# The linear part of an MLP, associated the other way: (h w_in) first instead of w_in (alpha w_out)

## The chip, the cores and the metric

The kernel runs on one core of a Trainium2 chip. The time is device microseconds of one execution; the median of 3 runs is shown. Engines: PE is TensorE, ACT ScalarE, DVE VectorE, POOL GpSimd, SP the engine that issues the DMAs.

## What is computed

The input x has 12480 rows (tokens) of 128 values. An attention with 32 inducing rows comes first, then two MLPs with 2048 hidden values:

```python
h = mab(I, x)                  # 32 rows attend to all of x: h is 32 x 128
x = mab(x, h)                  # each token attends to the 32 rows: a @ h, a is 12480 x 32
h1 = x @ w_in                                                    # first MLP
x = (np.maximum(h1, 0) + alpha * np.minimum(h1, 0)) @ w_out
r = np.maximum(x @ w2_in, 0)                                     # second MLP
out = (r * r) @ w2_out
```

`mab` is softmax(q kv^T / sqrt(128)) kv. All is fp32; w_in, w_out, w2_in and w2_out come as float64 and alpha has 2048 values.

## The kernel before

The first MLP's activation is split as alpha h1 + (1 - alpha) max(h1, 0). The second part needs the hidden layer; the first one is linear. With x = a h, the linear part is a V with V = h w_in diag(alpha) w_out, a matrix of 32 x 128 that is made once. `aw` holds first (1 - alpha) w_out, which is split in a high and a low part (`wo_hi`, `wo_lo`), and later alpha w_out.

*Stage 1* (to about 38 us) reads x, transposes it and gathers h over tokens. h is kept transposed and four times side by side: `hT`, 128 x 128 (L429). During this stage w_in is brought to fp32 (`w_in_sb`), and w_out behind it in four pieces (`convs[4]` to `convs[7]`: ACT, ACT, DVE, DVE and POOL, then `rest` and `split`).

*Between the stages* stand the scores and softmax of token tile 0 (`first`, steps 0 to 7) and of tiles 1 to 3 (`second`, steps 0 to 6), and `make_w1s(k)`: four products that give w1s = h w_in, 512 columns each. In the kernel before, PE also transposes the 16 chunks of w_in (`transpose_w_in(0..3)`, L388 to L393), and ACT copies them to `wiT`.

*The main loop* goes over s = 0 to 479. Step s computes chunk c = s mod 16 of token tile s // 16. `l1_a` multiplies a tile's attention weights `a_s` with w1s, ACT and DVE make the high and low part of max(h1, 0) (`g1h`, `g1l`); some steps later `l1_b` multiplies them with `wo_hi` and `wo_lo`, three products, and adds them up in a bank `y`. From step 24 on `l2_a`, `l2_split` and `l2_b` do the second MLP, whose weights arrive and are converted in eight pieces during the first steps (`PIECES`). Each engine works in order, and the order is written out by hand: `at(s, f)` hangs f behind step s. So were hung, in the kernel before:

- `second[2]` to `second[6]` (softmax of tiles 1 to 3) at steps 0, 2, 2, 4 and 7. `second[6]` makes `a_hi` on ACT and `a_lo` on POOL, and twelve DMAs on SP copy them to `a_s` of three tiles. Behind these twelve in SP's queue stands the load of the first piece of w2_out (step 9).
- `make_w1s(2)` at step 2 and `make_w1s(3)` at step 5.
- The scaling of `aw` by alpha on ACT (L219) at steps 8, 7, 16 and 15 (`AW`), and `step_u(0..3)` at steps 16 to 19: u = w_in (alpha w_out), 16 products summed in one bank.
- `copy_u` on ACT at 19, `step_v` at 20 (the product of `hT` and u on PE, L580, then `v_s` on ACT and DVE), and `end_y1(0)` at 22, which adds a V to tile 0 and is the first to read `v_s`.

PSUM has eight banks by name: h1 two, h2 two, y1 one, y2 two, ms one. Banks of one name are used in turn, and a new use waits until the last reader of the use before it (two uses before, for a pair) is done.

Of the kernel before, what the change touches and what calls it, by code (L numbers as in the profile page):

```python
# [9 lines left out]
F32 = mybir.dt.float32  # L10
# [3 lines left out]
AF = mybir.ActivationFunctionType  # L14
ALU = mybir.AluOpType
# [10 lines left out]
Q = 4  # L26
# [3 lines left out]
def attention_then_two_mlps(ctx: ExitStack, tc, x, inducing, w_in, w_out, alpha, w2_in, w2_out, out):  # L30
# [13 lines left out]
    scale = 1.0 / math.sqrt(C)  # L44
# [6 lines left out]
    keep = ctx.enter_context(tc.tile_pool(name="keep", bufs=1))  # L51
# [21 lines left out]
    def keep_tile(name, shape, dt=F32):  # L73
        return keep.tile(shape, dt, name=name, tag=name)
# [8 lines left out]
    def st_tile(name, shape):  # L83
        return st.tile(shape, F32, name=name, tag=name)
# [11 lines left out]

    ident = cv.tile([P, P], F32, name="ident", tag="u_sb", bufs=1)
    make_identity(nc, ident)  # L100

    same = st_tile("same", [P, P])
    nc.gpsimd.memset(same, 0.0)
    for k in range(-(Q - 1), Q):
        nc.gpsimd.affine_select(
# [19 lines left out]

    w_in_sb = keep.tile([P, DFF], F32, name="w_in_sb", tag="w2i_hi")
    w_out_sb = keep.tile([P, NCH, P], F32, name="w_out_sb", tag="w2i_lo")
    wiT = keep.tile([P, DFF], F32, name="wiT", tag="w2o_hi")
    aw = keep.tile([P, NCH, P], F32, name="aw", tag="w2o_lo")
    al = keep_tile("al", [P, NCH])  # L130
    al1 = keep_tile("al1", [P, NCH])
# [43 lines left out]
    def to_f32(name, k, place):  # L175

        v = {}  # L180
# [27 lines left out]
    def conv_w_out(k):  # L208
        chunks, cols = slice(4 * k, 4 * k + 4), slice(k * 512, (k + 1) * 512)
        f, hi, lo, a = (v.rearrange("p c d -> p (c d)")[:, cols] for v in (w_out_sb, wo_hi, wo_lo, aw))  # L210

        def rest():
            nc.gpsimd.tensor_tensor(
                aw[:, chunks], w_out_sb[:, chunks], al1[:, chunks].unsqueeze(2).to_broadcast([P, 4, P]), op=ALU.mult
            )

        def scaled():
            for c in range(4 * k, 4 * k + 4):
                nc.scalar.activation(aw[:, c, :], w_out_sb[:, c, :], AF.Copy, scale=al[:, c : c + 1])  # L219

        def split():
            nc.scalar.copy(hi, a)
            pool_lo(lo, a, hi)


        return to_f32("w_out", k, lambda: f) + [rest, split, scaled]

    def conv_w2(name, k, hi, lo):
        f = []
# [129 lines left out]
    b = free_bank()  # L359
# [25 lines left out]
            nc.vector.tensor_copy(al, b[:, :NCH])  # L385
            nc.vector.tensor_scalar(al1, al, -1.0, 1.0, op0=ALU.mult, op1=ALU.add)

    def transpose_w_in(k):  # L388
        b = y2_bank()
        for i in range(4):  # L390
            c = 4 * k + i
            nc.tensor.transpose(b[:, i * P : (i + 1) * P], w_in_sb[:, c * P : (c + 1) * P], ident)
        nc.scalar.copy(wiT[:, k * 512 : (k + 1) * 512], b)  # L393


    b = scores(last)
    values1(last - 1)
    maxima(last, b)
# [24 lines left out]
    den = st.tile([P, M], F32, name="den", tag="den")  # L423
    nc.vector.tensor_scalar_add(den, d[:, :M], 1e-9)
    nc.vector.reciprocal(den, den)
    transpose_w_in(0)
    b = y1_bank()
    nc.tensor.matmul(b[:, :P], h_run, sel, start=True, stop=True)
    nc.vector.tensor_tensor(  # L429
        hT.rearrange("c (q j) -> c q j", q=Q), b[:, :P].rearrange("c (q j) -> c q j", q=Q),  # L430
        den.unsqueeze(1).to_broadcast([P, Q, M]), op=ALU.mult,
    )
    transpose_w_in(1)
    run(convs[5][2:4])
    convs[4][4]()

# [99 lines left out]
    second = second_attention([1, 2, 3])  # L536
    first[0]()
    make_w1s(0)
    transpose_w_in(2)
    run(convs[6][:2])  # L540
    run(first[1:4])
    split_w1s(0, 0)
    second[0]()
    transpose_w_in(3)
    stage1.close()
    make_w1s(1)
    convs[5][4]()
# [12 lines left out]

    u_bank = []

    def step_u(k):
        if k == 0:
            u_bank.append(y2_bank())
        for c in range(4 * k, 4 * k + 4):
            nc.tensor.matmul(
                u_bank[0][:, :P], wiT[:, c * P : (c + 1) * P], aw[:, c, :], start=(c == 0), stop=(c == NCH - 1)  # L570
            )

    u_sb = cv.tile([P, P], F32, name="u_sb", tag="u_sb", bufs=1)

    def copy_u():
        nc.scalar.copy(u_sb, u_bank[0][:, :P])

    def step_v():
        bv = free_bank()
        nc.tensor.matmul(bv[:, :P], hT, u_sb, start=True, stop=True)  # L580
        nc.scalar.copy(v_s, bv[:, :P])
        nc.vector.tensor_tensor(v_s[64:], bv[64:, :P], f32(v_s[64:]), op=ALU.subtract)

# [98 lines left out]
    def at(s, f, *a):  # L682
        plan.setdefault(s, []).append(lambda: f(*a))
# [108 lines left out]
```

## Time and profile before

| | us |
|---|---|
| median of 3 runs | 978.12 (977.93 to 978.18) |
| the profiled execution | 976.3 |
| its span, first to last instruction | 974.2 |
| PE busy in the span | 957.3 (98%) |
| ACT busy | 756.1 (78%) |
| DVE busy | 671.8 (69%) |
| POOL busy | 543.7 (56%) |

The times in a timeline count from the span's start. Where a row carries "[1.29 <-ACT u_sb L576]", the engine had been idle for 1.29 us before it, and what ended this was that instruction. Matmuls overlap, so that the duration of one is longer than its distance to the next. An f32 product is two passes in the timeline. Buffer numbers are left out of names, so the arrays of the second MLP (`moe2`) read like those of the first.

### The profile page before, as it was taken

To read this page: it belongs to the slowest core of one execution; us is meant where nothing else is said; L and a number is where in the kernel's file an instruction comes from. 1 tells how busy PE (TensorE), PEld (TensorE's weight loads), DVE (VectorE), ACT (ScalarE), POOL (GpSimd) and SP (SyncE) were. 2 spreads that over 40 slices of the span, in tenths; PEclk is the share of its full clock that TensorE was granted. 3 is DMA by queue.
4 is the path that set the end of the run, shared out by engine and by line. 5 is a ranking of instruction groups with operands and counts; after the bars stand their busy time and mean duration, and the time that the engine had idled before them with its cause. 6 is when DMAs were issued, how large, how long until landed. Compare 5 with 4: busy or idle time off the path is not lost.

```text
span 974.2 us, 15106 instructions
## 1 busy us (share of the span) xinstructions
PE 957.3 (98%) x5023; PEld 879.7 (90%) x5023; DVE 671.8 (69%) x1129; ACT 756.1 (78%) x1500; POOL 543.7 (56%) x484
## 2 busy tenths in 40 slices
PE   9889999999999999999999999999999999999997
PEld 7568999998999989999999999899998999999997
DVE  5778876666766667666677666676666766666677
ACT  5689887777877777777788777787777787777775
POOL 2358765555665555655556555566555665555530
PEclk9999999999999999999999999999999999999999
DMA  9531002000020000110000200002000010000001
GB/s 327 155 101 59 9 3 46 11 10 1 10 48 10 1 10 10 30 20 10 10 10 3 46 11 10 1 11 48 10 1 10 10 34 16 10 10 10 1 10 20
DMA packets 65838, 28.36 MB, mean 29 GB/s; under 512 B 53968, under 2 KB 61664, under 8 KB 65760
## 3 DMA queue, kind: packets, MB, share of 16 engines
q1 hardware_dynamic: 64832, 27.29, 11.3%
q8 instruction: 39, 0.64, 0.3%
q14 instruction: 39, 0.32, 0.1%
q10 hardware_dynamic: 928, 0.11, 0.1%
HBM read 14.80 MB, written 6.39 MB: 22 GB/s over the span
## 4 chain that ended last, share of the span: by engine, by line
PE 93%; DMA 2%; DVE 2%; ACT 2%; issue 1%; SPq 0%; ACTq 0%; DVEq 0%
PE y L604 18%; PE y L605 18%; PE y L606 18%; PE h L604 9%; PE h L606 9%; PE h L605 9%; PE h L594 9%; DMA xg<-in_x_dram 2%; PE y L622 1%; PE ms L453 1%; DVE g1l L600 1%; DMA raw<-in_moe_w_out_dram 0%; ACT g1h L598 0%; PE h L262 0%; PE ms L276 0%
## 5 line engine op out<-in xcount | busy, mean ns | idle before, releaser
L649 POOL TENSOR_TENSOR g2l<-sq,g2h 128x448 fp32r<-128x448 f32 (+1 forms) x424 | 486.4, 1148 | 343.8 <-ACT g2h L647 336.5
L600 DVE SCALAR_TENSOR_TENSOR g1l<-h,g1h 128x448 fp32r<-128x448 f32 (+1 forms) x448 | 277.3, 620 | 226.0 <-ACT g1h L598 220.6
L598 ACT ACTIVATE g1h<-h 128x448 fp32r<-128x448 f32 (+1 forms) x448 | 243.7, 545 | 135.4 <-PE h L594 131.7
L640 DVE TENSOR_TENSOR sq<-h,r 128x448 f32<-128x448 f32 (+1 forms) x448 | 278.1, 621 | 49.0 <-ACT r L638 4.8
L638 ACT ACTIVATE r<-h 128x448 f32<-128x448 f32 (+1 forms) x448 | 244.5, 546 | 54.2 <-PE h L606 8.7
L647 ACT CAST g2h<-sq 128x448 fp32r<-128x448 f32 (+1 forms) x448 | 249.4, 557 | 1.8 <-DVE sq L640 1.5
L594 PE MATMUL h<-a_s,w1s 128*128 128x448 f32 (+1 forms) x448 | 164.6, 368 | 4.8 <-DVE g1l L600 3.1
L604 PE MATMUL h<-y1h,w2i_hi 128*128 128x448 f32 (+1 forms) x448 | 162.8, 363 | 0.1
L606 PE MATMUL y<-g1l,wo_hi 128*128 128x448 f32 (+1 forms) x448 | 162.4, 363 | 0.0
L606 PE MATMUL h<-y1l,w2i_hi 128*128 128x448 f32 (+1 forms) x448 | 162.2, 362 | 0.2 <-DVE y1l L626 0.2
L604 PE MATMUL y<-g1h,wo_hi 128*128 128x448 f32 (+1 forms) x448 | 162.4, 362 | 0.0
L605 PE MATMUL y<-g1h,wo_lo 128*128 128x448 f32 (+1 forms) x448 | 162.3, 362 | 0.0
L606 PE MATMUL y<-g2l,w2o_hi 128*128 128x448 f32 (+1 forms) x448 | 162.2, 362 | 0.0
L604 PE MATMUL y<-g2h,w2o_hi 128*128 128x448 f32 (+1 forms) x448 | 162.2, 362 | 0.0
L605 PE MATMUL y<-g2h,w2o_lo 128*128 128x448 f32 (+1 forms) x448 | 162.1, 362 | 0.0
L605 PE MATMUL h<-y1h,w2i_lo 128*128 128x448 f32 (+1 forms) x448 | 162.1, 362 | 0.0
L594 PEld LDWEIGHTS h<-a_s,w1s 128*128 128x128 f32 (+1 forms) x448 | 84.1, 188 | 17.3 <-DVE g1l L600 6.3
L604 PEld LDWEIGHTS h<-y1h,w2i_hi 128*128 128x128 f32 x448 | 84.1, 188 | 7.2 <-DVE sq L640 1.4
L604 PEld LDWEIGHTS y<-g1h,wo_hi 128*128 128x128 f32 x448 | 84.4, 188 | 5.6 <-issue 0.5
L606 PEld LDWEIGHTS h<-y1l,w2i_hi 128*128 128x128 f32 x448 | 84.1, 188 | 5.8 <-DVE y1l L626 0.5
L606 PEld LDWEIGHTS y<-g2l,w2o_hi 128*128 128x128 f32 x448 | 84.1, 188 | 5.7 <-DVE g2l L649 0.2
L604 PEld LDWEIGHTS y<-g2h,w2o_hi 128*128 128x128 f32 x448 | 84.1, 188 | 5.6
(124 smaller groups left out, 723.0 us busy)
## 6 DMA issues: line engine op xcount, KB each, us to landing
out_dram<-o SPq DMA_DIRECT2D x106, 56.0 KB, 1.9
xg<-in_x_dram SPq DMA_DIRECT2D x10, 512.0 KB, 8.8
raw<-in_moe_w_in_dram SPq DMA_DIRECT2D x8, 512.0 KB, 6.3
raw<-in_moe_w_out_dram SPq DMA_DIRECT2D x8, 512.0 KB, 4.2
a_s<-a_hi SPq DMA_DIRECT2D x54, 56.0 KB, 1.9
a_s<-a_lo SPq DMA_DIRECT2D x54, 56.0 KB, 1.9
xg<-in_x_dram SPq DMA_DIRECT2D x4, 256.0 KB, 4.2
out_dram<-o SPq DMA_DIRECT2D x4, 48.0 KB, 1.8
```

The costliest lines, as they stand in the source:

```text
L453: nc.tensor.matmul(b[i * M : (i + 1) * M, :w], hT[:, :M], rhs, start=True, stop=True, tile_position=(0, i * M),)
L594: nc.tensor.matmul(b[:, :w], w1s[: a.shape[0], c * P : (c + 1) * P], a, start=True, stop=True)
L598: nc.scalar.activation(hi, b[:, :w], AF.Relu)
L600: nc.vector.scalar_tensor_tensor(lo, b[:, :w], 0.0, f32(hi), op0=ALU.max, op1=ALU.subtract)
L604: nc.tensor.matmul(b, w_hi, hi, start=start, stop=False)
L605: nc.tensor.matmul(b, w_lo, hi, start=False, stop=False)
L606: nc.tensor.matmul(b, w_hi, lo, start=False, stop=stop)
L622: nc.tensor.matmul(b, v_s[: a.shape[0]], a, start=False, stop=True)
L638: nc.scalar.activation(r, b, AF.Relu)
L640: nc.vector.tensor_tensor(sq, b, r, op=ALU.mult)
L647: nc.scalar.copy(hi, sq)
L649: (nc.vector if i >= total - LAG2 else nc.gpsimd).tensor_tensor(lo, sq, f32(hi), op=ALU.subtract)
```

## The change

V is associated the other way. Sixteen products with a chunk of `w_in_sb` as weights and the 32 columns of `hT` as the moving side give (h w_in) transposed, chunk by chunk, in one bank (`step_wa`, step 0). DVE scales it by alpha into `wa` (`scale_wa`, step 4). Then sixteen products with `wa` (128 x 32) as weights and `w_out_sb` as the moving side go to four column groups of the array (`step_v(0..3)`, steps 16 to 19). Four partial sums stand one below the other in the bank, and a product with `same` (1 where two indices agree modulo 32) adds them and repeats the sum four times (`split_v`, step 20, in place of `step_v`). The transposes of w_in, `wiT`, the scaling on ACT and u go.

```diff
-    def transpose_w_in(k):
-        b = y2_bank()
-        for i in range(4):
-            c = 4 * k + i
-            nc.tensor.transpose(b[:, i * P : (i + 1) * P], w_in_sb[:, c * P : (c + 1) * P], ident)
-        nc.scalar.copy(wiT[:, k * 512 : (k + 1) * 512], b)
...
-        def scaled():
-            for c in range(4 * k, 4 * k + 4):
-                nc.scalar.activation(aw[:, c, :], w_out_sb[:, c, :], AF.Copy, scale=al[:, c : c + 1])
...
-    def step_u(k):
+    wa = att.tile([P, NCH, M], F32, name="wa", tag="wa")
+    wa_bank, v_bank = [], []
+
+    def step_wa():
+        wa_bank.append(y2_bank())
+        for c in range(NCH):
+            nc.tensor.matmul(
+                wa_bank[0][:, c * M : (c + 1) * M], w_in_sb[:, c * P : (c + 1) * P], hT[:, :M], start=True, stop=True
+            )
+
+    def scale_wa():
+        nc.vector.tensor_tensor(
+            wa, wa_bank[0].rearrange("p (c j) -> p c j", j=M), al.unsqueeze(2).to_broadcast([P, NCH, M]), op=ALU.mult
+        )
+
+    def step_v(k):
         if k == 0:
-            u_bank.append(y2_bank())
+            v_bank.append(y2_bank())
         for c in range(4 * k, 4 * k + 4):
+            q = c % Q
             nc.tensor.matmul(
-                u_bank[0][:, :P], wiT[:, c * P : (c + 1) * P], aw[:, c, :], start=(c == 0), stop=(c == NCH - 1)
-            )
...
+                v_bank[0][q * M : (q + 1) * M, :P], wa[:, c, :], w_out_sb[:, c, :],
+                start=(c < Q), stop=(c >= NCH - Q), tile_position=(0, q * M),
+            )
...
+    def split_v():
         bv = free_bank()
-        nc.tensor.matmul(bv[:, :P], hT, u_sb, start=True, stop=True)
+        nc.tensor.matmul(bv[:, :P], same, v_sb, start=True, stop=True)
...
+    at(0, step_wa)
+    at(4, scale_wa)
     for k in range(4):
-        at(AW[k], convs[4 + k][6])
-        at(16 + k, step_u, k)
-    at(19, copy_u)
-    at(20, step_v)
+        at(16 + k, step_v, k)
+    at(19, copy_v)
+    at(20, split_v)
```

The calls of `transpose_w_in` go from four places between the stages. `same` is kept past stage 1, and `w2_out`'s high part no longer shares its place with `wiT`.

On PE, from the first products of the main loop to the start of `make_w1s(3)`. Before: the products of chunks 0, 1 and 2 (L594), `make_w1s(2)` (L526, bank y_752), chunks 3 to 5, the first `l1_b`, `make_w1s(3)` (y_792). "waits" names the engines whose counters a row waits for.

```order
L594 MATMUL h_728<-a_s,w1s 128x384 [waits DVE_49]
L594 MATMUL h_739<-a_s,w1s 128x384
L594 MATMUL h_746<-a_s,w1s 128x384
L526 MATMUL y_752<-w_in_sb,hT 128x512 [waits PE_49]
L594 MATMUL h_763<-a_s,w1s 128x384 [waits DVE_49]
L594 MATMUL h_771<-a_s,w1s 128x384 [waits DVE_49,Activation_49]
L594 MATMUL h_779<-a_s,w1s 128x384
L604 MATMUL y_785<-g1h,wo_hi 128x384 [waits Activation_49]
L605 MATMUL y_785<-g1h,wo_lo 128x384 [waits Pool_49]
L606 MATMUL y_785<-g1l,wo_hi 128x384
L526 MATMUL y_792<-w_in_sb,hT 128x512
L594 MATMUL h_795<-a_s,w1s 128x384 [waits DVE_49]
```

After, the rows from the last three of `step_wa`'s sixteen products (L552), which stand between chunk 0 and chunk 1; line numbers are those of the changed kernel, and `make_w1s` is L511.

```order
L552 MATMUL y_715<-hT,w_in_sb 128x32 x3
L592 MATMUL h_732<-a_s,w1s 128x384
L592 MATMUL h_739<-a_s,w1s 128x384
L511 MATMUL y_745<-w_in_sb,hT 128x512 [waits PE_49]
L592 MATMUL h_756<-a_s,w1s 128x384 [waits DVE_49]
L592 MATMUL h_764<-a_s,w1s 128x384 [waits DVE_49,Activation_49]
L592 MATMUL h_773<-a_s,w1s 128x384
L602 MATMUL y_779<-g1h,wo_hi 128x384 [waits Activation_49]
L603 MATMUL y_779<-g1h,wo_lo 128x384 [waits Pool_49]
L604 MATMUL y_779<-g1l,wo_hi 128x384
L511 MATMUL y_786<-w_in_sb,hT 128x512 [waits DVE_49]
L592 MATMUL h_789<-a_s,w1s 128x384
```

Chunks 1 and 2 and `make_w1s(2)` have moved behind `step_wa`, and `make_w1s(3)` (y_786) now waits for DVE.

On ACT, between the stages, from the weight of the last partial sums (`wgt`) on. Before: the conversions (L186, L189), three copies to `wiT`, two more conversions, the exponential of tile 0 (L470).

```order
L414 ACTIVATE wgt<-ms,nnm 128x1
L186 ACTIVATE mag<-raw 128x512
L189 ACTIVATE raw<-raw 128x512
L393 COPY wiT<-y_641 128x512
L393 COPY wiT<-y_650 128x512
L393 COPY wiT<-y_666 128x512
L186 ACTIVATE mag<-raw 128x512
L189 ACTIVATE raw<-raw 128x512
L470 ACTIVATE a_675<-a_675 96x128
L533 CAST w1s<-h_664 128x512
L393 COPY wiT<-y_686 128x512
```

After:

```order
L401 ACTIVATE wgt<-ms,nnm 128x1
L185 ACTIVATE mag<-raw 128x512
L188 ACTIVATE raw<-raw 128x512
L185 ACTIVATE mag<-raw 128x512
L188 ACTIVATE raw<-raw 128x512
L455 ACTIVATE a_656<-a_656 96x128
L518 CAST w1s<-h_651 128x512
L217 CAST wo_hi<-aw 128x512
```

The copies to `wiT` are gone, and the conversions and the exponential have moved up.

On DVE, at steps 3 to 5, around the transpose of the weights of tiles 1 to 3 to `a2t`. Before:

```order
L600 SCALAR_TENSOR_TENSOR g1l<-h_763,g1h 128x384
L600 SCALAR_TENSOR_TENSOR g1l<-h_771,g1h 128x384
L483 STREAM_TRANSPOSE a2t<-a_717 96x448
L600 SCALAR_TENSOR_TENSOR g1l<-h_779,g1h 128x384
L531 TENSOR_TENSOR w1s<-y_752,w1s 64x512
L193 TENSOR_SCALAR mag<-mag 128x512
```

After:

```order
L598 SCALAR_TENSOR_TENSOR g1l<-h_756,g1h 128x384
L598 SCALAR_TENSOR_TENSOR g1l<-h_764,g1h 128x384
L468 STREAM_TRANSPOSE a2t<-a_692 96x448
L557 TENSOR_TENSOR wa<-y_715,al 128x512
L598 SCALAR_TENSOR_TENSOR g1l<-h_773,g1h 128x384
L516 TENSOR_TENSOR w1s<-y_745,w1s 64x512
```

`scale_wa` (L557) stands directly behind that transpose, ahead of the low part of chunk 5.

## Rows read from the trace of the kernel before

**Rows 1.** The page's chain that ended last, shares of the span by engine

```profile
PE 93%; DMA 2%; DVE 2%; ACT 2%; issue 1%; SPq 0%; ACTq 0%; DVEq 0%
```

**Rows 2.** Timeline of PE: start, us, engine, line, op, out<-in, count [idle before]

```profile
35.34 1.08 PE L337 MATMUL y<-xg,eT 128*32 128x128 f32 x32 [0.28 <-ACT eT L330]
...
38.44 0.41 PE L421 MATMUL ms<-sel,s_run 128*128 128x32 f32 x2
38.69 0.64 PE L392 MATMUL y<-ident,w_in_sb 128*128 128x128 f32 x4
...
47.62 0.79 PE L594 MATMUL h<-a_s,w1s 96*128 96x384 f32 x3 [1.34 <-DVE a_s L516]
48.25 1.02 PE L526 MATMUL y<-w_in_sb,hT 128*128 128x512 f32 x2
51.78 0.44 PE L594 MATMUL h<-a_s,w1s 96*128 96x384 f32 x1 [2.51 <-DVE g1l L600]
...
54.09 1.91 PE L526 MATMUL y<-w_in_sb,hT 128*128 128x512 f32 x2
...
64.73 1.05 PE L569 MATMUL y<-aw,wiT 128*128 128x128 f32 x8
65.54 0.45 PE L594 MATMUL h<-a_s,w1s 128*128 128x448 f32 x1
...
73.12 0.49 PE L580 MATMUL ms<-u_sb,hT 128*128 128x128 f32 x2 [1.29 <-ACT u_sb L576]
```

**Rows 3.** Timeline of ACT, the same columns

```profile
41.97 0.58 ACT L393 COPY wiT<-y 128x512 f32<-128x512 f32 x1 [1.37 <-PE y L392]
...
43.60 0.29 ACT L470 ACTIVATE a<-a 96x128 f32<-96x128 f32 x1
...
49.75 0.60 ACT L533 CAST w1s<-y 128x512 fp32r<-128x512 f32 x1
51.29 0.58 ACT L470 ACTIVATE a<-a 96x448 f32<-96x448 f32 x1 [0.95 <-DVE a L467]
...
57.50 0.55 ACT L492 CAST a_hi<-a2t 96x448 fp32r<-96x448 f32 x1
57.95 1.28 ACT L219 ACTIVATE aw<-w_out_sb,al 128x128 f32<-128x128 f32 x4
...
70.83 0.68 ACT L186 ACTIVATE mag<-raw 128x512 f32<-128x512 f32 x1 [0.96 <-DMA raw<-in_moe_w_out_dram]
...
72.81 0.26 ACT L576 COPY u_sb<-y 128x128 f32<-128x128 f32 x1
```

**Rows 4.** Timeline of SP's DMA issues

```profile
59.30 0.51 SPq L498 DMA_DIRECT2D a_s<-a_lo  x1
...
66.67 0.53 SPq L168 DMA_DIRECT2D raw<-in_moe_w_out_dram  x1
```

**Rows 5.** Timeline of DVE

```profile
41.51 1.00 DVE L467 TENSOR_TENSOR a<-a,mx 96x128 f32<-96x128 f32 x1
...
44.67 0.29 DVE L479 TENSOR_TENSOR a<-a,sm 96x128 f32<-96x128 f32 x1
...
45.33 0.69 DVE L531 TENSOR_TENSOR w1s<-h,w1s 64x512 fp32r<-64x512 f32 x1
...
52.96 0.61 DVE L475 TENSOR_REDUCE sm<-a 96x14 f32<-96x448 f32 x1
...
55.16 0.64 DVE L483 STREAM_TRANSPOSE a2t<-a 96x448 f32<-96x448 f32 x1 [0.24 <-POOL a L479]
```

**Rows 6.** Timeline of POOL

```profile
41.07 1.29 POOL L198 TENSOR_TENSOR w_out_sb<-mag,raw 128x512 int32<-128x512 int32 x1 [4.80 <-ACT wiT L393]
42.32 2.09 POOL L213 TENSOR_TENSOR aw<-w_out_sb,al 128x512 f32<-128x512 f32 x2
```

**Rows 7.** Stretches: us, busy of PE, PEld, DVE, ACT, POOL; granted clock, DMA share, GB/s

```profile
53.00:54.00 1.00, 1.00 (x5) 1.00 (x4) 0.93 (x5) 1.00 (x4) 0.00 (x0) 0.50 0.00 0
74.00:76.00 2.00, 2.00 (x12) 1.68 (x11) 1.84 (x4) 2.00 (x6) 1.20 (x2) 1.00 0.03 10
```

More of the change, by code (lines that the diff above doesn't have):

```diff
@@ L95, in attention_then_two_mlps @@
     keep_busy(5)
-    ident = cv.tile([P, P], F32, name="ident", tag="u_sb", bufs=1)
+    ident = cv.tile([P, P], F32, name="ident", tag="v_sb", bufs=1)
     make_identity(nc, ident)
-    same = st_tile("same", [P, P])
+    same = keep_tile("same", [P, P])
     nc.gpsimd.memset(same, 0.0)
@@ L127, in attention_then_two_mlps @@
     w_out_sb = keep.tile([P, NCH, P], F32, name="w_out_sb", tag="w2i_lo")
-    wiT = keep.tile([P, DFF], F32, name="wiT", tag="w2o_hi")
     aw = keep.tile([P, NCH, P], F32, name="aw", tag="w2o_lo")
@@ L223, in split @@
             pool_lo(lo, a, hi)
-        return to_f32("w_out", k, lambda: f) + [rest, split, scaled]
+        return to_f32("w_out", k, lambda: f) + [rest, split]
     def conv_w2(name, k, hi, lo):
@@ L425, in attention_then_two_mlps @@
     nc.vector.reciprocal(den, den)
-    transpose_w_in(0)
     b = y1_bank()
@@ L432, in attention_then_two_mlps @@
     )
-    transpose_w_in(1)
     run(convs[5][2:4])
@@ L538, in attention_then_two_mlps @@
     make_w1s(0)
-    transpose_w_in(2)
     run(convs[6][:2])
@@ L543, in attention_then_two_mlps @@
     second[0]()
-    transpose_w_in(3)
     stage1.close()
@@ L559, in attention_then_two_mlps, with copy_v @@
     load_w("w2_in", 1)
-    u_bank = []
-    def step_u(k):
+    wa = att.tile([P, NCH, M], F32, name="wa", tag="wa")
[11 more added lines that the diff above has]
+    def step_v(k):
         if k == 0:
-            u_bank.append(y2_bank())
+            v_bank.append(y2_bank())
         for c in range(4 * k, 4 * k + 4):
+            q = c % Q
             nc.tensor.matmul(
-                u_bank[0][:, :P], wiT[:, c * P : (c + 1) * P], aw[:, c, :], start=(c == 0), stop=(c == NCH - 1)
-            )
[L573 to L578, printed above, removed]
+                v_bank[0][q * M : (q + 1) * M, :P], wa[:, c, :], w_out_sb[:, c, :],
+                start=(c < Q), stop=(c >= NCH - Q), tile_position=(0, q * M),
+            )
+    v_sb = cv.tile([P, P], F32, name="v_sb", tag="v_sb", bufs=1)
+    def copy_v():
+        nc.scalar.copy(v_sb, v_bank[0][:, :P])
+    def split_v():
         bv = free_bank()
-        nc.tensor.matmul(bv[:, :P], hT, u_sb, start=True, stop=True)
+        nc.tensor.matmul(bv[:, :P], same, v_sb, start=True, stop=True)
         nc.scalar.copy(v_s, bv[:, :P])
@@ L673, in attention_then_two_mlps @@
     LAG1, LAG1_EARLY, LAG2, LAG2B, EARLY = 3, 5, 24, 4, 20
-    AW = [8, 7, 16, 15]
     PIECES = [
```

## The prediction

> **What bounds the kernel now.** I read the shares of the chain that ended last first, then the timelines of the engines between 30 and 92 us, then the granted clock in short stretches. The chain is TensorE (PE) for 93% of the span [rows 1], so from afar only PE's own work seems to count. The timelines show that this is not so where the change lies. Between 38 and 74 us PE stands still four times for others: 2.51 us for VectorE (DVE), 1.29 us for the copy of u on ScalarE (ACT), and twice more in between [rows 2]. After 92 us the view of waits lists none for PE. Whatever this ramp loses or gains is therefore seen at the end, one for one.
>
> The wait of 1.29 us is the one to follow back, since everything after it hangs on it. The copy `u_sb` (L576) runs at 72.81, because ACT had stood idle until 70.83 for the load of the first piece of the second MLP's w_out, and it works in order [rows 3]. That load was issued on SP at 66.67, at the end of a queue of twelve copies of `a_s` of which the second starts at 59.30 [rows 4]; it landed 4.14 us later. The queue starts when `a_hi` (L492, 57.50) and then `a_lo` are there [rows 3]. So the chain that sets the end of the ramp is: `a_hi`, the SP queue, the load, ACT, the small product L580 at 73.12. If `a_hi` moves by some amount, the end of the program moves by it, and PE work saved between 56 and 72 us only lengthens the 1.29 us.
>
> **The change part by part.** *Removed ahead of the loop.* Sixteen transposes on PE (L392, four in 0.64 us) and four copies of `wiT` on ACT. They don't sit on the path themselves, but the third copy (41.97) holds two weight conversions and, behind these, the exponential of the first tile (L470, 43.60) [rows 2, 3]. ACT is now free for the conversions from 39.2 on, and the exponential can follow DVE's subtraction L467, which ends at 42.51 [rows 5]: 1.1 us earlier. Part of that is taken back. L467 took 1.00 us where L479, of the same size, takes 0.29, and it ended 0.15 us after GpSimd's (POOL) L198 [rows 5, 6]: the two engines' element-wise work on SBUF excludes each other. L479 would now come at 43.6, inside POOL's two L213 (42.32 to 44.41), and end near 44.5 instead of 44.96, 0.46 us earlier. The gain at the first `g1` product (L594, 47.62) is between 0.46 and 1.1; I take 0.6, so 47.0.
>
> *Added at step 0: `step_wa`.* Sixteen products with full 128x128 weights and 32 moving columns, each two passes as every f32 product here: 32 passes. The row of the same shape is L421: its second pass and the next product follow it by 0.25 us for two, 0.125 each. Of L569 (same weights, 128 columns) eight take 0.81 us, 0.10 each. The least that the trace shows is L337, with weights of 32 columns: 32 passes in 1.08 us, 0.034 each [rows 2]. So it costs between 1.1 and 4.0 us; I take 0.11 a pass, 3.5 us, between the two rows with full weights. PE was idle for 2.51 us here, so half of it looks free, but what is queued behind it is not: the products of chunks 1 and 2 (0.2 us each) and `make_w1s(2)` (1.02 us) [rows 2], and behind this on ACT its cast L533 and then the exponential of the next three tiles (L470, 51.29) [rows 3]. From 47.2: `step_wa` ends at 50.7, `make_w1s(2)` at 52.1, the cast at 52.6, the exponential at 53.2. DVE's L475 then starts at 53.25; before, 52.96 [rows 5]. The 0.6 us gained have become 0.3 us lost.
>
> *Added at step 4: `scale_wa` on DVE*, directly behind the transpose to `a2t`. It reads a PSUM bank of 512 columns, and the nearest row is L531 with 0.69 us [rows 5] (L479 gives the low end, 0.29; L467, held by POOL, the high end, 1.00). L475 to the end of `a2t` (55.80) keeps its 2.84 us, so `a2t` ends at 56.1 and `wa` at 56.8.
>
> *The new wait.* `make_w1s(3)` takes a bank of the pair y2, and the bank two before it is now that of `wa`. Before, it started at 54.09 without a wait [rows 2]; the order of the changed kernel has a wait for DVE there. It starts at 56.8. Then it takes 1.02 us at the full clock, against the 1.91 us before, when the granted clock was 0.50 [rows 2, 7]: it ends at 57.8 instead of 56.0. PE and ACT do the same as before from there, so the cast of the last `w1s`, two `g1h` and `a_hi` come 1.7 to 1.8 us later (a tenth is regained by the clock): `a_hi` at 59.2.
>
> *Then* the twelve copies, the load and ACT come 1.7 us later, and L580 at 74.8.
>
> *`step_u` becomes `step_v`.* 32 passes in groups of eight of 0.81 us (64.73 to 65.54), 3.2 us, become 32 passes with weights of 32 columns, 1.1 us by L337 [rows 2]. On ACT sixteen scalings go (four in 1.28 us, L219) [rows 3]. None of it is on the path named above: PE did what lay between 56.0 and 71.83 in 15.8 us and now needs at most 13.7, so it stands ready at 71.5 or sooner, and waits over 3 us for the small product where it waited 1.29. L580 itself keeps its size, with `same` in place of `hT`. POOL's `w2i_lo` now waits for the last of `step_v`, near 71, where POOL wrote it from about 70.6 on; PE wants it only after L580, so this is covered by the same wait, and it would cost only if it were over 4 us late.
>
> *The clock.* After the idle 2.51 us the granted clock was 0.50, and `make_w1s(3)` took 0.9 us more than `make_w1s(2)`; after the idle 1.29 us it stayed at 1.00 [rows 2, 7]. The change makes two idle stretches that are longer than both: about 3 us ahead of `make_w1s(3)` (the products before it end near 53.9) and over 3 us ahead of L580. Whether one gives a slow stretch can't be read here; I price each with 0.9 us and take one of the two.
>
> Sum: +1.7 +0.9 = +2.6 us. It is made on the profiled execution (976.3 us, of which 974.2 are the span); the median of the runs shown is 978.12, 1.8 above, and I add the sum to that: 980.7 us. Without any slow stretch it is 979.8.
>
> **The rivals.** *Both idle stretches are followed by a slow clock*: +1.7 +1.8 = +3.5, 981.6 us. For it: each is longer than the one after which the clock fell. Against: PE may be ahead of DVE and ACT after L580, and then a slow PE costs less.
>
> *`step_wa` is short* (not slower). If a pass with 32 columns takes 0.034 us, `step_wa` ends at 48.3 and `make_w1s(2)` at 49.7, and the exponential is again set by DVE: 51.29 - 0.6 = 50.7. Then `a2t` ends at 55.2, `wa` at 55.9, `make_w1s(3)` at 56.9 at the full clock, and `a_hi` moves by only +0.8: 978.9 us; with the full 1.1 us gained at the start, 978.4. It decides from a pass of about 0.06 us downwards, where the exponential no longer waits for PE. Against it: the 0.25 us for the two passes of L421. The Trainium skill, "TensorE: Matmul & The Clock Gate", section "Back-to-back issue gap", gives about 60 cycles, 25 ns, for anything of 1 to 64 columns; by this 32 passes would be an estimated 0.8 us, and the time that of this rival. The trace does not agree, with 125 ns, though in two passes only.
>
> *PE's own work decides.* PE has 93% of the chain. The transposes (at most 4 x 0.64 = 2.6 us) and 3.2 us go, 1.1 and 3.5 us come: -1.2, 976.9 us; with a short `step_wa`, -3.6, 974.5 us. Against it: ACT's wait for the load at 70.83 is no matter of PE.
>
> **How the numbers follow.** Forecast (the new wait carries through to the end) 0.40; both slow stretches 0.22; short `step_wa` 0.24; PE's work alone 0.14. From no change one can tell about 0.2%, 1.96 us, so slower means over 980.08 and faster under 976.16. Of the forecast 0.02 lies below 980.08 (no slow stretch, a low price of a pass), which leaves 0.38 slower, and 0.22 from the second: 0.60. Same: 0.02 + 0.24 + 0.06 of PE's work = 0.32. Faster: 0.08. The range goes from 977.5 (short `step_wa` with a cheap scaling) to 983.0 (passes of 0.125 us, +0.5, and both slow stretches with one of them dearer); the forecast's own range is 979.8 to 981.5.
>
> **What would show it.** In the trace after: the exponential of the first tile near 42.5; the passes of `step_wa` from 47.2 over about 3.5 us; the next tiles' exponential not before 52; PE idle for about 3 us until `wa` is written, and `make_w1s(3)` ending near 57.8 or later; `a_hi` near 59; ACT still waiting for the load of w_out, near 72.5; and an idle stretch of over 3 us ahead of the small product. I am wrong if passes of 32 columns run at 0.06 us or less, if `a_hi` comes before 57.5, or if the wait ahead of L580 has shrunk.

## The result

The changed kernel takes 990.1 us (median of 4 runs, 989.23 to 990.47), the kernel before 978.02 us beside it (977.65 to 978.18): a ratio of 1.0133, 95% interval 1.012 to 1.0145. It is slower, as forecast, but by 12.1 us where 2.6 were forecast; 990.1 lies outside the range. The profiled execution took 990.18 us with a span of 988.1, which is 13.9 more than the span before. The profiled execution of the kernel before was 1.7 us faster than the median of its runs, so that the spans lie further apart than the medians.

### Where the 13.9 us are

The output of each token tile ends with one transpose on DVE. The first and the last of the 28 divide the span into a ramp and a steady part. The view of the tile `o`, first of the kernel before, then of the changed one (count, least, median and most ns, first and last start in us):

```profile
L664 DVE STREAM_TRANSPOSE o<-y x28: 572/640/649, 116.7 to 968.9; 128x448 f32<-128x448 f32 x27, 128x384 f32<-128x384 f32 x1
```

```profile
L662 DVE STREAM_TRANSPOSE o<-y x28: 574/640/650, 125.3 to 982.9; 128x448 f32<-128x448 f32 x27, 128x384 f32<-128x384 f32 x1
```

The first comes 125.3 - 116.7 = 8.6 us later. From the first to the last it takes 982.9 - 125.3 = 857.6 us instead of 852.2: another 5.4 us, 0.20 for each of 27 tiles. There are two losses, then, and the prediction spoke of one.

### The ramp after

Line numbers are two lower than before in the loop, and up to fifteen lower in the attention ahead of it. Its timeline of PE, which answers to [rows 2]:

```profile
44.99 0.91 PE L492 MATMUL y<-a2t,same_q 96*128 96x128 f32 x6 [1.70 <-DVE a2t L468]
...
47.04 0.44 PE L592 MATMUL h<-a_s,w1s 96*128 96x384 f32 x1 [1.15 <-DVE a_s L501]
47.32 5.85 PE L552 MATMUL y<-hT,w_in_sb 128*128 128x32 f32 x32
...
53.77 1.91 PE L511 MATMUL y<-w_in_sb,hT 128*128 128x512 f32 x2
...
60.37 2.07 PE L511 MATMUL y<-w_in_sb,hT 128*128 128x512 f32 x2 [2.77 <-DVE wa L557]
...
79.80 0.79 PE L578 MATMUL ms<-v_sb,same 128*128 128x128 f32 x2 [3.03 <-ACT v_sb L574]
```

`step_wa` (L552) stands ahead of `make_w1s(2)` (53.77) and took 5.85 us. `make_w1s(3)` (60.37) waited 2.77 us for `wa`, a wait that the kernel before does not have. DVE's timeline, which answers to [rows 5], shows what it waited for:

```profile
43.62 0.88 DVE L464 TENSOR_TENSOR a<-a,sm 96x128 f32<-96x128 f32 x1
...
59.11 0.63 DVE L468 STREAM_TRANSPOSE a2t<-a 96x448 f32<-96x448 f32 x1
59.66 0.65 DVE L557 TENSOR_TENSOR wa<-y,al 128x512 f32<-128x512 f32 x1
```

ACT's timeline, which answers to [rows 3]:

```profile
42.49 0.31 ACT L455 ACTIVATE a<-a 96x128 f32<-96x128 f32 x1 [2.23 <-DVE a L452]
...
55.71 0.58 ACT L518 CAST w1s<-y 128x512 fp32r<-128x512 f32 x1 [1.16 <-PE y L511]
56.19 0.58 ACT L455 ACTIVATE a<-a 96x448 f32<-96x448 f32 x1
...
64.47 0.55 ACT L477 CAST a_hi<-a2t 96x448 fp32r<-96x448 f32 x1
...
77.51 0.66 ACT L185 ACTIVATE mag<-raw 128x512 f32<-128x512 f32 x1 [2.78 <-DMA raw<-in_moe_w_out_dram]
```

The exponential of the next three tiles (56.19) stands on ACT behind the cast of `make_w1s(2)`, and the cast waited for PE. `a_hi` comes at 64.47, 6.97 later than before. From there the delay is handed on almost unchanged. SP's issues, which answer to [rows 4]:

```profile
66.27 0.51 SPq L483 DMA_DIRECT2D a_s<-a_lo  x1
...
73.22 0.53 SPq L167 DMA_DIRECT2D raw<-in_moe_w_out_dram  x1
```

The load is 6.55 us later, ACT's work behind it 6.68, the small product 6.68. The last 1.9 us of the 8.6 are lost behind that product. The stretches of the changed kernel (us, busy time of PE, PEld, DVE, ACT and POOL, granted clock, DMA share, GB/s), which answer to [rows 7]:

```profile
48.00:49.00 1.00, 1.00 (x9) 1.00 (x8) 1.00 (x3) 0.52 (x2) 1.00 (x1) 0.72 0.00 0
49.00:57.00 8.00, 8.00 (x29) 6.78 (x29) 3.65 (x6) 2.16 (x5) 2.72 (x3) 0.50 0.00 0
57.00:60.00 3.00, 0.60 (x2) 0.09 (x1) 2.60 (x7) 2.54 (x6) 1.96 (x2) 0.50 0.00 0
60.00:65.00 5.00, 4.63 (x11) 3.60 (x12) 2.85 (x6) 1.90 (x4) 0.21 (x1) 0.50 0.01 3
...
80.00:85.00 5.00, 5.00 (x15) 4.52 (x16) 4.00 (x9) 4.08 (x9) 2.68 (x2) 0.50 0.14 54
```

The clock went to 0.50 (1.2 in place of 2.4 GHz) while `step_wa` ran, stayed there for some 17 us although PE was busy for 8 of 8 us from 49 to 57, and went down once more at the small product. The kernel before had one such stretch of about 3 us. Of its two idle stretches ahead of the main loop, [rows 2] has the one of 1.34 us; the other one is this, which answers to L492 above:

```profile
45.35 0.93 PE L507 MATMUL y<-a2t,same_q 96*128 96x128 f32 x6 [1.09 <-DVE a2t L483]
```

### The steady part after

Some of the products of 448 columns between 200 and 900 us, by line and names (count, busy us, mean ns of one, idle before). The kernel before:

```profile
L604 PE MATMUL y<-g2h,w2o_hi 128*128 128x448 f32 x345 | 125.2, 363 | 0.0
L606 PE MATMUL y<-g1l,wo_hi 128*128 128x448 f32 x345 | 125.2, 363 | 0.0
```

The changed kernel:

```profile
L603 PE MATMUL y<-g2h,w2o_lo 128*128 128x448 f32 x343 | 125.8, 367 | 0.0
L604 PE MATMUL y<-g1l,wo_hi 128*128 128x448 f32 x343 | 125.8, 367 | 0.0
L604 PE MATMUL y<-g2l,w2o_hi 128*128 128x448 f32 x343 | 125.5, 366 | 0.0
L602 PE MATMUL y<-g2h,w2o_hi 128*128 128x448 f32 x343 | 125.5, 366 | 0.0
...
L602 PE MATMUL y<-g1h,wo_hi 128*128 128x448 f32 x343 | 124.3, 362 | 0.0
```

Four of the ten products of a step are longer by 3 to 4 ns, with no idle time and the same instructions. From the starts in the trace, those four are followed by the next product after 203.1 to 203.3 ns, the other six, as all ten before, after 200.0 to 200.2. 4 x 16 x 3.2 ns = 0.20 us per token tile, the whole of the second loss. They are the products during which `w2o_hi` is loaded, and those next to them. The diff does not change how `w2o_hi` is used, but it removes `wiT`, which had claimed that buffer early: in the changed kernel it is laid out last, at byte 117,440 of a partition, where before it lay between `w2i_lo` and `w2o_lo`. Also, `wa` and `same` push the working tiles up by 2,560 B.

### The profile page after: what moved, and what is told of

It is laid out like the page before. It is cut to its first block, busy times and chain, and to the rows that moved or that the text cites. A ratio compares the mean times of both kernels' runs of the same rounds, so it can differ in the third digit from the quotient of the medians.

```text
span 988.1 us, 15118 instructions
## 1 busy us (share of the span) xinstructions
PE 968.7 (98%) x5039; PEld 886.1 (90%) x5039; DVE 673.2 (68%) x1130; ACT 750.2 (76%) x1480; POOL 544.6 (55%) x484
## 4 chain that ended last, share of the span: by engine, by line
PE 93%; DMA 2%; DVE 2%; SPq 1%; issue 1%; ACT 1%; POOL 0%; ACTq 0%; DVEq 0%; POOLq 0%
PE y L604 18%; PE y L603 18%; PE y L602 18%; PE h L602 9%; PE h L604 9%; PE h L603 9%; PE h L592 9%; DMA xg<-in_x_dram 2%; SPq L483 1%; PE y L620 1%; PE y L552 1%; PE ms L438 1%; DMA raw<-in_moe_w_out_dram 0%; PE h L257 0%; PE ms L271 0%
## 5 line engine op out<-in xcount | busy, mean ns | idle before, releaser
L592 PE MATMUL h<-a_s,w1s 128*128 128x448 f32 (+1 forms) x448 | 166.9, 374 | 1.4 <-DVE a_s L501 1.1
L604 PE MATMUL y<-g1l,wo_hi 128*128 128x448 f32 (+1 forms) x448 | 165.0, 368 | 0.0
L603 PEld LDWEIGHTS y<-g2h,w2o_lo 128*128 128x128 f32 x448 | 84.6, 189 | 6.7
L603 PEld LDWEIGHTS y<-g1h,wo_lo 128*128 128x128 f32 x448 | 85.1, 190 | 5.4
```

The source lines that it names most:

```text
L592: nc.tensor.matmul(b[:, :w], w1s[: a.shape[0], c * P : (c + 1) * P], a, start=True, stop=True)
L603: nc.tensor.matmul(b, w_lo, hi, start=False, stop=False)
L604: nc.tensor.matmul(b, w_hi, lo, start=False, stop=stop)
```

## The experiments

Three theories could explain the loss in the steady part: the place of `w2o_hi`, the shift of the working tiles, or the order of instructions. Two could explain the longer ramp: the place of `step_wa` in the order with the wait that it brings, or the clock, brought down either by idle time of PE or by the small passes. Since the start of the attention varies by up to 2.8 us between executions, ramps are compared from the moment when `hT` is written (DVE) to the first output transpose, one profiled execution each:

| kernel | `hT` | `a_hi` | first transpose | from `hT` | first to last |
|---|---|---|---|---|---|
| before | 39.58 | 57.50 | 116.7 | 77.1 | 852.2 |
| changed | 39.53 | 64.47 | 125.3 | 85.8 | 857.6 |
| p_shift | 39.25 | 57.72 | 116.5 | 77.3 | 852.6 |
| p_claim | 39.55 | 64.03 | 125.2 | 85.7 | 852.7 |
| p_align | 42.05 | 67.37 | 128.7 | 86.6 | 874.1 |
| p_off | 39.77 | 63.22 | 124.0 | 84.2 | 852.7 |
| e_fill | 39.80 | 61.26 | 121.8 | 82.0 | 857.6 |
| e_one | 42.04 | 63.51 | 124.9 | 82.8 | 857.6 |
| e_ms | 40.32 | 62.03 | 121.5 | 81.2 | 857.6 |
| e_step2 | 40.18 | 56.63 | 116.2 | 76.0 | 852.6 |
| e_load | 39.77 | 58.44 | 115.4 | 75.6 | 852.7 |

The changed kernel, p_claim, p_align and p_off have the same order of products on PE, and their ramps go from 84.2 to 86.6 us. A difference of some 2 us between two single ramps is therefore not a finding by itself.

### p_shift: the kernel before, its tiles moved

```
-    same = st_tile("same", [P, P])
+    same = keep_tile("same", [P, P])
+    spare = att.tile([P, NCH, M], F32, name="spare", tag="spare")
+    nc.gpsimd.memset(spare[:1, :1, :1], 0.0)
```

> The kernel before, with its own instructions, and only the places of its tiles changed: same lies in the lasting pool and a tile of 2,048 B that only one 4-byte memset writes lies in the pool of wa. So the lasting tiles stand 512 B and the working tiles of the main loop (g1h to o) 2,560 B further up, as in the changed kernel, but w2o_hi keeps its neighbour's place between w2i_lo and w2o_lo. Theory 'shift' (the 0.20 us per token tile that the changed kernel loses in its steady part come from where the working tiles lie): output transposes 32.41 us apart, ramp as before, 978.0 + 5.4 = 983.4 us. Theory 'weights' place' (they come from w2o_hi, which the changed kernel puts at the end of the lasting pool) and theory 'program' (from the changed order of instructions): 32.21 us apart, 978.0 us, within 0.5.

976.95 us, the kernel before 977.06 beside it: ratio 0.9995 (0.9984 to 1.0005); 852.6 us from the first to the last transpose. The shift costs nothing. The run shows something else by the way: this program has the instructions of the kernel before, but its granted clock was low for longer.

```profile
47.00:57.00 10.00, 8.47 (x18) 5.49 (x19) 9.48 (x18) 6.82 (x14) 6.12 (x6) 0.50 0.00 0
```

Ten us at half clock, and the first transpose still at 116.5 us. In the order of the kernel before, a slow clock here falls into time in which PE waits anyway.

### p_claim: the changed kernel, w2o_hi in its old place

```
     w_out_sb = keep.tile([P, NCH, P], F32, name="w_out_sb", tag="w2i_lo")
+    claim = keep.tile([P, DFF], F32, name="claim", tag="w2o_hi")
     aw = keep.tile([P, NCH, P], F32, name="aw", tag="w2o_lo")
```

> The changed kernel, with one line more: an unused tile claims the buffer of w2o_hi where wiT did, so that w2o_hi lies between w2i_lo and w2o_lo again; no instruction is added. Theory 'weights' place': output transposes 32.21 us apart again, the first of them still at about 125.3 us, 990.1 - 5.3 = 984.8 us. Theories 'shift' and 'program': 32.41 us apart, 990.1 us, within 0.5.

983.52 us, 1.0057 (1.0039 to 1.0076) of the kernel before. The view of the tile `o`:

```profile
L663 DVE STREAM_TRANSPOSE o<-y x28: 573/641/650, 125.2 to 977.9; 128x448 f32<-128x448 f32 x27, 128x384 f32<-128x384 f32 x1
```

977.9 - 125.2 = 852.7 us: the steady part is that of before, the ramp that of the changed kernel. (The profiled execution is the slowest of five, 985.22; they go down to 980.49, so that the loss differs from run to run.) This settles the second loss: it comes from where `w2o_hi` lies.

### e_fill: work in the idle stretches ahead of step_wa

```
+    def fill(n):
+        b = h1_bank()
+        for _ in range(n):
+            nc.tensor.matmul(b[:, :P], ident, ident, start=True, stop=True)
...
+    fill(6)
     first[6]()
...
+    fill(4)
     for s in range(total + LAG2 + LAG2B + 4):
```

> The changed kernel, with products of 128 columns (ident times ident, results unused) in the two idle stretches of PE ahead of step_wa: six ahead of the small spread products (idle 43.2 to 45.0 us) and four ahead of the first product of the main loop (idle 45.9 to 47.0 us). Theory 'idle' (the granted clock falls to 0.50 at 48.5 us because PE stood still before): the clock stays at 1.00 through step_wa, its 32 passes end after 3.4 us by the rate at which the first of them ran, the exponential of tiles 1 to 3 comes near 52.7 instead of 56.2 us, the product that forms v_s at about 75 to 76 instead of 79.8 us, in all 984 to 986 us. Theory 'small passes' (the passes of 32 columns themselves bring it down, whatever stood before): 0.50 from about 48.5 us on as in the changed kernel, step_wa 5.8 us, 990 us, within 1.

986.33 us, 1.0098 (1.0076 to 1.012); the ramp is 3.8 us shorter than in the changed kernel and 2.2 us shorter than the shortest with that order. PE's timeline and two stretches:

```profile
43.40 1.50 PE L523 MATMUL h<-ident 128*128 128x128 f32 x12
...
46.00 1.06 PE L523 MATMUL h<-ident 128*128 128x128 f32 x8
...
47.59 3.65 PE L558 MATMUL y<-hT,w_in_sb 128*128 128x32 f32 x32
```

```profile
46.00:52.00 6.00, 5.74 (x46) 5.26 (x45) 4.43 (x7) 2.42 (x6) 3.86 (x3) 0.98 0.00 0
52.00:55.00 3.00, 3.00 (x8) 1.75 (x6) 2.48 (x5) 2.21 (x6) 0.08 (x1) 0.50 0.02 5
```

With the idle time filled, `step_wa` ran at the full clock: 3.65 us, 0.114 a pass. The half clock came all the same, behind it, from 51.8 to 55.2 us and again from 58.6 to 62.0. In this execution it was later and shorter than in the changed kernel; it was not gone. The theory of idle time gets `step_wa` right and the total within 0.4 us, but not this late stretch: the next tiles' exponential came at 53.69 for 52.7.

### e_one: one dense product in place of the 32 passes

```
-        for c in range(NCH):
-            nc.tensor.matmul(
-                wa_bank[0][:, c * M : (c + 1) * M], w_in_sb[:, c * P : (c + 1) * P], hT[:, :M], start=True, stop=True
-            )
+        nc.tensor.matmul(wa_bank[0], hT, w_in_sb[:, :512], start=True, stop=True)
```

> The changed kernel, but step_wa is one product of 512 columns (hT against the first 512 columns of w_in_sb) into the same bank at the same place, in place of its 32 passes; so wa is not what the reference wants, and every wait stays. Theory 'small passes': the clock stays at 1.00 where it fell at 48.5 us, the product takes 0.9 us, the exponential of tiles 1 to 3 comes near 50 us (51.29 before the change), the product that forms v_s near 72.5 us (73.12 before), the ramp is no longer than before; only the loss per token tile is left, 983 us within 1. Theory 'idle': the clock falls to 0.50 in or right behind that product all the same, and stays there into the sixties; the exponential near 52.5 us, the product for v_s near 76 us, 986 to 988 us.

987.53 us, 1.0108 (1.0088 to 1.0128). `hT` came 2.5 us late in the profiled execution, so what counts is 82.8 us from there: 2.9 less than the changed kernel, 5.7 more than before.

```profile
50.46 1.91 PE L551 MATMUL y<-w_in_sb,hT 128*128 128x512 f32 x2
...
59.41 2.08 PE L511 MATMUL y<-w_in_sb,hT 128*128 128x512 f32 x2 [3.34 <-DVE wa L554]
```

The clock fell without small passes, already at 47.8 us, in the products L492 behind 1.69 us of idle PE; so the theory of the small passes falls. And with 4 us less work in that place most of the loss stays, together with a wait of 3.34 us for `wa`.

### e_ms: the new wait taken away

```
-        wa_bank.append(y2_bank())
+        wa_bank.append(ms_bank())
```

> The changed kernel, but wa's products go to the one bank ms, which nothing else uses until step 20, instead of one of the two y2 banks: make_w1s(3) no longer waits for scale_wa; the 32 passes of step_wa stay where they are. Theory 'carried wait' (most of what a_hi is late by comes from that wait, whose 2.8 us of idle PE come on top of the late exponential): the product of make_w1s(3) near 57.7 instead of 60.4 us, a_hi at 60.3 to 61 instead of 64.5 us, the product that forms v_s near 76 instead of 79.8 us, in all 990.1 - 3.8 = 986.3 us. Theory 'clock alone' (what counts is only that PE runs at half clock from 48.5 us on): a_hi not before 63.5 us, 989 us or more. The output transposes stay 32.41 us apart by either.

986.25 us, 1.0099 (1.0081 to 1.0117), 0.05 us off what the carried wait gives. That closeness is luck, as the rows show. PE and ACT:

```profile
49.31 5.25 PE L552 MATMUL ms<-hT,w_in_sb 128*128 128x32 f32 x32 [1.05 <-DVE a L446]
...
58.47 1.02 PE L511 MATMUL y<-w_in_sb,hT 128*128 128x512 f32 x2
...
77.92 0.49 PE L578 MATMUL ms<-v_sb,same 128*128 128x128 f32 x2 [1.26 <-ACT v_sb L574]
```

```profile
62.03 0.58 ACT L477 CAST a_hi<-a2t 96x448 fp32r<-96x448 f32 x1
```

`step_wa` was slow again (5.25 us, and 1.05 late for its new bank), and `a2t` was no earlier than in the changed kernel. Still `a_hi` comes 21.7 us after `hT` in place of 24.9, and the first transpose after 81.2 in place of 85.8. At 62.03 `a_hi` is later than the 60.3 to 61 expected, 0.8 of it because `hT` was, and the small product comes at 77.92 where 76 was expected. What makes up for this is that no half clock follows it: the first transpose comes 43.6 us behind it, as before the change, not 45.5 as in the changed kernel. The 3.2 us that `a_hi` gains are not the wait alone, either: `make_w1s(3)` started 3.2 us before `wa` was written (61.7), but the clock was also back at 1.00 from 58.1 us on, so that it took 1.02 us in place of 2.07. The wait is on the path; its share can't be told from that of the clock to better than about 1 us.

### e_step2: step_wa behind make_w1s(2)

On top of the edits of p_claim and e_ms:

```
-    at(0, step_wa)
-    at(4, scale_wa)
+    at(2, step_wa)
+    at(8, scale_wa)
```

> The changed kernel with three edits: w2o_hi's buffer claimed early (the steady part of before, 32.21 us per token tile), wa in the bank ms, and step_wa at step 2, behind make_w1s(2), in place of step 0, scale_wa at step 8. In the kernel before, PE stands idle behind make_w1s(2) from 49.3 to 51.8 us. Theory 'place in the order' (what makes the ramp long is that step_wa stands ahead of the next tiles' exponential and of make_w1s(3)): that exponential near 50.8 us, a_hi 57.0 to 57.5 us, the product for v_s at or before 73.1 us, 976.5 to 978 us, no longer than the kernel before. Theory 'clock' (wherever they stand, the passes make PE slow for some 15 us and everything behind late): the granted clock at 0.50 from near 50 to beyond 60 us, a_hi at 59 us or later, the product for v_s at 75 us, 980 us or more.

977.36 us, the kernel before 976.93 beside it: 1.0012 (0.9987 to 1.0036), so no loss is left that is clear of the noise. The ten runs go from 974.34 to 984.21 us, though; the profiled one took 976.06.

```profile
48.30 1.02 PE L512 MATMUL y<-w_in_sb,hT 128*128 128x512 f32 x2
49.17 3.73 PE L553 MATMUL ms<-hT,w_in_sb 128*128 128x32 f32 x32
...
53.88 1.02 PE L512 MATMUL y<-w_in_sb,hT 128*128 128x512 f32 x2
...
72.61 0.49 PE L579 MATMUL ms<-v_sb,same 128*128 128x128 f32 x2 [2.70 <-ACT v_sb L575]
```

The 32 passes run where PE stood idle for 2.51 us before the change [rows 2], and take 3.73 us. The stretches from 44 to 92 us all show a granted clock of 1.00, through the passes and behind them. `a_hi` comes 16.5 us after `hT`, 1.5 earlier than before the change. But in this execution the half clock came ahead of the main loop (us, busy time of PE, granted clock, DMA share, GB/s):

```profile
42.00:44.00 2.00, 2.00 (x8) 0.50 0.07 12
```

So it is not shown what a half clock during the passes would cost at this place; the slower ones of the ten runs may be such executions. Nor was the move to step 2 run with `wa` in its first bank.

### e_load: and the load ahead of the copies

```
-    at(9, load_w, *PIECES[2][1:])
+    at(6, lambda: load_w(*PIECES[2][1:]))
     at(7, second[6])
```

> The version with step_wa at step 2, wa in the bank ms and w2o_hi in its old place, and the load of the first piece of w2_out put on SP's queue ahead of the twelve copies into a_s (step 6, before second[6], in place of step 9). In the version without this last edit ACT waits 2.4 us for that load, and PE 2.7 us for v_sb behind it. Theory 'load behind the copies' (the ramp now ends with that load): ACT does not wait there, the product that forms v_s comes 2 to 2.5 us earlier (near 70.3 us by the same start), 975 us, faster than both kernels by 2 us. Theory 'traded wait' (the twelve copies then come later by what the load takes on the queue, and the scores or the next conversion wait instead): the same product early, but the first product with g2h as before, 977 us.

973.59 us, the kernel before 976.50 beside it: 0.9984 (0.9967 to 1.0000). It beats the changed kernel by 16 us. That it beats the kernel before, as expected, is not shown: nine of its twelve runs lie from 972.8 to 975.8 us and three from 978.8 to 980.3, and the interval reaches 1. SP's issues and PE:

```profile
50.39 0.38 SPq L168 DMA_DIRECT2D raw<-in_moe_w_out_dram  x1
59.02 0.60 SPq L484 DMA_DIRECT2D a_s<-a_hi  x1
```

```profile
70.97 0.49 PE L579 MATMUL ms<-v_sb,same 128*128 128x128 f32 x2 [0.21 <-ACT v_sb L575]
```

PE's wait for `v_sb` goes from 2.70 to 0.21 us. The first transpose gains only 0.4 on e_step2 when counted from `hT`; in this execution the clock was at 0.50 from 39.6 to 46.5 us and from 53.3 to 56.7 us, and `a_hi` came about two us later than there, so what the load is worth alone is not settled by one profile.

### p_align, p_all, p_off, p_move: what it is in the place

These runs add pads that nothing reads, before and behind tiles. `p_align` and `p_off` are the changed kernel; the lines are those of `p_align`, with `p_off`'s sizes behind #:

```
+            nc.vector.memset(keep_tile("pad", [P, 8]), 0.0)    # p_off: 56
             w2.extend(keep.tile([P, DFF], F32R, name=v, tag=v) for v in ("w2o_hi", "w2o_lo"))
+            nc.vector.memset(keep_tile("pad2", [P, 24]), 0.0)  # p_off: 72
```

`p_all` and `p_move` are the kernel before, with a pad of 32 B ahead of `w1s` and one of 96 B behind `indT` (a small tile behind the weights), or with one of 128 B behind `indT` alone.

> The changed kernel with two unused pads (32 and 96 B) around w2o_hi's buffer: it starts at byte 117,472 in place of 117,440 of each partition, 32 B past a multiple of 64 as all the other weight tiles are; the tiles behind it move by 128 B. Theory 'offset' (it costs time that w2o_hi alone starts on a multiple of 64 B): output transposes 32.21 us apart, 984.8 us. Theory 'region' (that it lies apart from the other weights, behind v_s and hT): 32.41 us, 990.1 us.

> The kernel before with a pad of 32 B ahead of the weight tiles and one of 96 B behind them: w1s, wo_hi, wo_lo and all four w2 tiles start on a multiple of 64 B, everything behind moves by 128 B. Theory 'offset': if every load of such a weight costs what the two loads of w2o_hi per step cost in the changed kernel (four products of 10 longer by 3.3 ns, 6.6 ns per load), ten loads cost 66 ns per step, 1.06 us per token tile of 16 steps: transposes 33.3 us apart, 978 + 29 = 1007 us. Theory 'mixed' (it costs only where weights of both offsets follow each other) and theory 'region': 32.21 us apart, 978 us.

1010.15 us and 997.73 us, one run each (the kernel before: 976.93): neither theory gave either. In p_align the two products during which `w2o_hi` is loaded are now the only ones that are not long, and eight others are:

```profile
L602 PE MATMUL y<-g2h,w2o_hi 128*128 128x448 f32 x337 | 124.2, 368 | 0.0
L604 PE MATMUL y<-g2l,w2o_hi 128*128 128x448 f32 x336 | 123.9, 369 | 0.0
...
L604 PE MATMUL y<-g1l,wo_hi 128*128 128x448 f32 x337 | 122.3, 363 | 0.0
...
L603 PE MATMUL y<-g2h,w2o_lo 128*128 128x448 f32 x337 | 122.1, 362 | 0.0
```

I had overlooked that the pads also move all working tiles by 128 B. The last two runs separate this.

> The changed kernel with unused pads of 224 and 288 B around w2o_hi's buffer: it stays at the end of the lasting pool, behind v_s and hT, but starts at byte 117,664, which is 416 beyond a multiple of 512 as all the other weight tiles are (117,440 is 192 beyond one), and the tiles behind it move by 512 B, which moved nothing else in the kernel with shifted places. Theory 'offset in 512' (the pitch depends on where in 512 B the weights that are being loaded lie): the four products around w2o_hi start 200 ns apart like the others, output transposes 32.21 us apart for a whole token tile, 5.3 us less than the changed kernel, 984.8 us. Theory 'region' (that it lies apart from the other weights): 203 ns, 32.41 us, 990.1 us.

> The kernel before with one pad of 128 B behind the weights: weight tiles and hT stay at their bytes, everything behind them (all moving operands of the main loop among them) lies 128 B further up. Theory 'distance' (what counts is the distance between the moving operand that is being read and the weights that are being loaded meanwhile; the two runs with pads moved both): with the distance that eight of ten products had in the first of them, 206.6 ns, all ten products start 206.6 instead of 200.0 ns apart, 160 x 6.6 ns = 1.06 us more per token tile, 977 + 28 = 1005 us. Theory 'weights alone' (what counts is where the weights lie): 200.0 ns, 977 us.

p_off (one run): 984.07 us, 976.7 - 124.0 = 852.7 us from first to last, and the four products are short again at the same end of the pool:

```profile
L604 PE MATMUL y<-g1l,wo_hi 128*128 128x448 f32 x346 | 125.5, 363 | 0.0
L602 PE MATMUL y<-g2h,w2o_hi 128*128 128x448 f32 x345 | 125.2, 363 | 0.0
```

p_move (one run): 1004.15 us (expected 1005), 877.9 us from the first to the last transpose, 25.7 more than before; the rest is that `hT` came 2.1 us later. With the weights where they were and the working tiles 128 B further up, all ten products of a step are long, 206.3 to 206.7 ns from start to start:

```profile
L607 PE MATMUL y<-g1l,wo_hi 128*128 128x448 f32 x335 | 123.7, 369 | 0.0
```

So it is neither the region nor the weights' offset alone, but the two offsets together.

## Why the prediction was right in sign and wrong in size

**What held.** The first exponential was due near 42.5 (42.49), the first `g1` product at 47.0 (47.04), with DVE's L464 held by POOL (0.88 us, forecast to end near 44.5; it ended at 44.50, POOL's L212 at 44.35). `make_w1s(3)` was to wait about 3 us for `wa` (2.77), and PE over 3 us ahead of the small product (3.03). The way from `a_hi` over SP's queue and the load to that product carried the delay through to within 0.3 us. e_ms shows that the new wait is on that path. Passes of 32 columns cost 0.114 to 0.117 us at the full clock (e_fill, e_step2), against 0.11 taken: the rival of a short `step_wa` is out. The Trainium skill, "TensorE: Matmul & The Clock Gate", section "Back-to-back issue gap", gives the 25 ns that the prediction quotes for the gap of a product by itself. For a stream in which each product has its own weight load, as here, the same section says that both set the spacing, and gives about 81 ns at 128 columns. The runs show 114 ns and more, and the measurement decides.

**The step that failed in the ramp** is "I price each with 0.9 us and take one of the two". It looked for slow clock only behind the two idle stretches that the change makes, and priced it by one product. What came was half clock from 48.4 us on, behind two idle stretches that were there before, too (1.70 and 1.15 us here; 1.09 and 1.34 in the kernel before). Before, 2.5 us of idle PE followed, and p_shift shows that even 10 us at half clock hid there. The change put 32 passes and everything behind them into that place, at once on the path: `step_wa` 5.85 us for 3.5, `make_w1s(2)` 1.91 for 1.02. `step_wa` was taken to end at 50.7 and ended at 53.2 (+2.5). The exponential was taken to end at 53.2 (the 53.2 of the prediction is an end, as its L475 at 53.25 shows) and ended at 56.8 (+3.6). `wa` was taken as written at 56.8 and was at 60.3 (+3.5). `make_w1s(3)` took 2.07 for 1.02, and `a_hi` came at 64.47 for 59.2 (+5.3). The small product came at 79.80 for the 74.8 without a slow stretch (+5.0). Then the slow stretch behind it cost about 1.9 for 0.9 (+1.0), and with this the ramp is 8.6 for 2.6. Of these 8.6 us, e_fill gives back 3.8, with the clock up during `step_wa`, and e_ms 4.6, without the wait, of which 1.9 come from the missing half clock behind the small product; the two overlap, since the wait is as long as PE is late. That both idle stretches are followed by a slow clock was the rival nearest to what happened, and it had the same price too low. Its first stretch can't be read in the changed kernel, where the clock was down already. In p_claim, e_fill and e_one the clock had come back, and it fell again during the wait for `wa` or within 1 us of its end (at 61.7, 58.6 and 58.1 us).

**The step that is missing** is the 5.4 us of the steady part. I took a removed tile, `wiT`, as removed work only, and did not ask whose buffer it was. No row of the profile of before has the price of this place, but the diff and the pools' order tell that `w2o_hi` moves. A hint was there: in the kernel before, the product during which `v_s` is loaded, from another offset, is followed after 204.9 ns, not 200.0.

**What stays open.** What brings the clock down at a given moment: it fell with and without the small passes, with and without filled idle time, and at 46.7 us (p_shift) or 52.9 us in the same instructions of the kernel before. The stretch at the small product is more regular. In the six profiled executions in which PE stood idle for 3.0 to 3.7 us ahead of that product (changed, p_claim, p_align, p_off, e_fill, e_one), the clock fell 0.6 to 1.1 us before the idle time ended, for 6.8 us; in the seven in which PE stood idle there for 0.2 to 2.7 us, it did not fall. This fits the theory that the idle time brings it down there, but no run changes that alone. Open is also the rule of the offsets (below).

## What to carry to other kernels

Work that fits into idle time of an engine is only free if nothing that others wait for is queued behind it: in the profiled executions, the same 32 passes came with 8.6 us of loss at step 0 and with none at step 2, behind the product that ACT wanted and in a bank of their own. When a ring of banks gets one more user, look at who takes the bank two allocations later, and give the new one a bank that is free for long. When a tile is added or removed, compare the addresses of all others before and after, as a change of layout can cost a steady loop more than the change itself.

## What the runs showed of the hardware that was not expected

In back-to-back products of 448 columns with 128x128 weights, the time from one start to the next depends on where the moving operand and the weights loaded meanwhile lie in a partition, though neither waits for anything. First bytes modulo 256, and the distance of starts, 294 to 345 pairs for each two products (21 for `v_s`):

| working tiles | weights being loaded | start to start |
|---|---|---|
| 64 | 160 (before, p_shift, p_claim, p_off) | 200.0 to 200.3 ns |
| 64 | 192 (`w2o_hi` in the changed kernel) | 203.2 to 203.3 |
| 64 | 32 (`v_s`, before) | 204.9 |
| 192 | 160 (p_align, p_move) | 206.3 to 207.4 |
| 192 | 224 (`w2o_hi` in p_align) | 199.3 to 199.5 |
| 192 | 192 (p_all) | 202.8 to 206.7 |

128 B of padding cost 25.7 us in this way, on 852 between the first and the last transpose (p_move). The table isn't a rule: in the changed kernel the loads of `w2o_lo` and `w1s` next to a `w2o_hi` product took 203.1 to 203.2 ns too, at an offset that is otherwise good, and no run tells why.

A granted clock of 0.50 lasted 17 us in the changed kernel, although PE was busy for all of the 8 us from 49 to 57 and for 4.63 of the 5 us from 60 to 65, and 10 us in p_shift, with PE busy for 8.47; both ended while PE went on with the same products as before.
